# Attention and routed experts on one core: eleven expert tiles start before the last sequence is dispatched

## The chip, the cores and the metric

The kernel runs on one core of one Trainium2 chip. The metric is device microseconds (us) of one execution. A core has TensorE (PE; the rows call its weight loads PEld), VectorE (DVE), ScalarE (ACT), GpSimd (POOL) and SyncE (SP), each with an instruction queue of its own that it works through in order. [...]

## The reference

Four sequences of 768 tokens, 8 heads of 64. First block-sparse attention: query block and key block (of 32) see each other if they are neighbours, if one of them is the first or last, or if the pair was drawn. Then each token goes to the one expert of eight whose embedding is nearest by cosine, and the expert's result is scaled by the gate.

```
scores = scale * q @ k.T;  scores = where(mask, scores, -1e9)
attn   = exp(scores - max) / (sum + 1e-9);  x = attn @ v          # 3072 tokens of 512
logits = (x / |x|) @ (emb / |emb|).T / tau                        # 8 experts
e = argmax(logits);  gate = softmax(logits)[e]
out = gate * (relu(x @ w1[e]) @ w2[e])                            # w1 512x1024, w2 1024x512
```

## The kernel before, in words

Everything is float32, with two matmul passes per product, so the rows count a float32 matmul twice.

**Attention** (`attention_fast`) is one loop over 192 units. Six units, one per 128 keys, make a window: a pair of heads and half of a sequence's queries. Eight windows make a sequence, 32 windows the whole. In unit u TensorE multiplies the exponentials `e` with the values into `av` (`attend_fast`, L311) and computes the scores `sc` of unit u+2 (`score_fast`, L290), of which ScalarE makes `e` (L293). DVE adds the `e` of a window into `esum` (L306, L308). At a window's end ScalarE copies half of `av` to `part` (L315) and DVE adds the other half into `at` (L317). That frees `av`, of which there is one. In the same place `turn_fast` transposes keys and queries of a later pair (L273) into a PSUM tile that DVE and ScalarE read as `kt` (L276) and `qt` (L277).

`settle` (L339, L346 and what follows) turns a finished window into rows of `x`: 12 matmuls `back<-back,at`, 24 matmuls that sum `esum`, then on DVE `dens`, `inv`, `x`, `part`, and `nsq` behind POOL's squares `sq` (L359). It is called in the second unit of the next window (u%6 == 1). After a sequence's last window come `route` (logits, arg-max `oh`, `gate`; a chain of small instructions on DVE, one on POOL, one on ScalarE), in unit 2, and `rank`, in unit 4: how many tokens before a token have the same expert. `rank` adds up `seen` on POOL (L451) and multiplies `rk` on TensorE (L453, L454). The last sequence does all three after the loop.

One PSUM tile, `small`, is shared by the transposes of a turn, `settle`, `rk`, `cp` and `slot_ps` (`two_banks`), one buffer in all.

**Dispatch** (L459) comes after the last `rank`: count per expert, tiles of 128 tokens per expert, a place for every token, and a matmul of one-hot rows that writes the token numbers into `slot`, 24 matmuls with `lane_oh` made on DVE in front of each.

**Experts.** 24 tiles, and up to 7 more behind conditions (three of those run). `fetch(i)` loads w1 and w2 of the tile's expert through SP, three buffers each, and gathers its 128 rows `xg` through POOL. `expert_tile` transposes `xg` (L553), copies it to `xgt` on DVE (L555), multiplies `hp` in two halves (L562), applies relu on ScalarE (L565) and DVE (L566), multiplies `yp` (L570) and scales it on DVE into `y` (L572), which POOL scatters.

The order on each engine is set by a scheduler of the language that lists the instructions by its own estimate of when they become ready. [...]

Of the kernel before, what the change touches and what calls it, by code (L numbers as in the profile page):

```python
# [10 lines left out]
F32 = mybir.dt.float32  # L11
# [7 lines left out]
P = 128  # L19
# [11 lines left out]
GS = G // P  # L31
NG = (N + E * (G - 1)) // G
NS = NG * GS
# [23 lines left out]
def build_consts(k):  # L57
# [342 lines left out]
def route(k, b):  # L400
# [18 lines left out]
    if not k.exact:  # L419
# [39 lines left out]
def dispatch(k):  # L459

    nc, p = k.nc, k.dp
    cp = two_banks(k, "cp")[:, 0]
    nc.tensor.matmul(cp[:, 0:E], lhsT=k.ones, rhs=k.seen[:, NT, :], start=True, stop=True)
    cnt = p.tile([P, E], F32, name="cnt")
    nc.vector.tensor_copy(out=cnt, in_=cp[:, 0:E])

    more = p.tile([P, E, N // G], F32, name="more")
    nc.vector.tensor_tensor(out=more, in0=cnt.unsqueeze(2).broadcast_to([P, E, N // G]),
                            in1=k.by_g.unsqueeze(1).broadcast_to([P, E, N // G]), op=ALU.is_gt)
    need = p.tile([P, E], F32, name="need")  # L470
    nc.vector.reduce_sum(out=need, in_=more, axis=AX.X)
    end = need
    for step in (1, 2, 4):
        nxt = p.tile([P, E], F32, name=f"end{step}")
        nc.vector.tensor_copy(out=nxt[:, 0:step], in_=end[:, 0:step])
        nc.vector.tensor_tensor(out=nxt[:, step:E], in0=end[:, step:E], in1=end[:, 0:E - step], op=ALU.add)
        end = nxt
# [3 lines left out]
    past = p.tile([P, NG, E], F32, name="past")  # L481
    nc.vector.tensor_tensor(out=past, in0=k.tile_no.unsqueeze(2).broadcast_to([P, NG, E]),
                            in1=end.unsqueeze(1).broadcast_to([P, NG, E]), op=ALU.is_ge)
    ex = p.tile([P, NG], F32, name="ex")
    nc.vector.reduce_sum(out=ex, in_=past, axis=AX.X)
    nc.vector.tensor_scalar(out=ex, in0=ex, scalar1=float(E - 1), scalar2=None, op0=ALU.min)
    k.expert = k.const.tile([P, NG], I32, name="expert")
    nc.vector.tensor_copy(out=k.expert, in_=ex)

# [15 lines left out]
    nc.vector.scalar_tensor_tensor(out=low, in0=hi, scalar=-float(P), in1=pos, op0=ALU.mult, op1=ALU.add)
# [246 lines left out]
```

## Time and profile before

| | us |
| --- | --- |
| median of 3 runs (873.19 to 874.57) | 873.22 |
| the profiled execution | 872.45 |
| its span, first to last instruction | 870.6 |
| TensorE busy | 774.4 |
| DVE busy | 328.3 |
| ACT busy | 200.0 |
| POOL busy | 101.1 |

The mean granted clock of TensorE is 0.957 of full speed. A window's row gives the length of a stretch, then busy time and number of instructions per engine. A line of the timeline gives start, duration and instruction, and in brackets how long the engine had idled before it and what ended that. Where one engine is busy for most of a stretch the reader looks for the releaser behind its remaining idle time.

### The profile page before, as it was taken

To read this page: it belongs to the slowest core of one execution; us is meant where nothing else is said; L and a number is where in the kernel's file an instruction comes from. 1 tells how busy PE (TensorE), PEld (TensorE's weight loads), DVE (VectorE), ACT (ScalarE), POOL (GpSimd) and SP (SyncE) were. 2 spreads that over 40 slices of the span, in tenths; PEclk is the share of its full clock that TensorE was granted. 3 is DMA by queue.
4 is the path that set the end of the run, shared out by engine and by line. 5 is a ranking of instruction groups with operands and counts; after the bars stand their busy time and mean duration, and the time that the engine had idled before them with its cause. 6 is when DMAs were issued, how large, how long until landed. Compare 5 with 4: busy or idle time off the path is not lost.

```text
span 870.6 us, 22250 instructions
## 1 busy us (share of the span) xinstructions
PE 774.4 (89%) x10030; PEld 504.6 (58%) x10030; DVE 328.3 (38%) x641; ACT 200.0 (23%) x292; POOL 101.1 (12%) x139
## 2 busy tenths in 40 slices
PE   5999979998799979997459999999999999999883
PEld 2555535555455545553447676767676767676661
DVE  3666656666566665666711111111111111110100
ACT  3545434444344434443000000000000000000000
POOL 2000010001100010001010111101010101010100
PEclk9999989999899989999559999999999999999997
DMA  5111131111111130000179999989999999988780
GB/s 200 39 42 50 43 128 58 57 57 58 74 57 57 58 129 20 3 3 2 72 290 399 399 398 323 330 312 324 323 315 323 322 322 321 326 314 314 272 296 28
DMA packets 63810, 162.31 MB, mean 186 GB/s; under 512 B 2956, under 2 KB 15244, under 8 KB 63190
## 3 DMA queue, kind: packets, MB, share of 16 engines
q1 hardware_dynamic: 58950, 146.45, 47.9%
q0 software_dynamic: 4480, 13.91, 4.0%
q8 instruction: 82, 1.34, 0.6%
q10 hardware_dynamic: 272, 0.39, 0.1%
q14 instruction: 26, 0.21, 0.1%
HBM read 148.14 MB, written 13.38 MB: 186 GB/s over the span
## 4 chain that ended last, share of the span: by engine, by line
PE 73%; DVE 9%; issue 6%; ACT 6%; DMA 2%; POOL 2%; SPq 0%; POOLq 0%; DVEq 0%; ACTq 0%
PE hp L562 20%; PE yp L570 19%; PE sc L290 14%; PE av L311 12%; ACT e L293 3%; DVE esum L306 3%; PE back L346 2%; PE back L339 2%; DVE kt L276 2%; ACT qt L277 2%; PE slot_ps L514 1%; PE xg_ps L553 1%; DMA xg<-x_dram,slot 1%; DMA out_dram<-y,slot 1%; POOL seen L451 1%
## 5 line engine op out<-in xcount | busy, mean ns | idle before, releaser
L562 PEld LDWEIGHTS hp<-xgt,w 128*128 128x128 f32 x1728 | 199.9, 193 | 25.2 <-issue 11.0
L562 PE MATMUL hp<-xgt,w 128*128 128x128 f32 x1728 | 204.7, 277 | 8.8 <-ACT h L565 4.6
L570 PE MATMUL yp<-w,h 128*128 128x512 f32 x432 | 189.9, 592 | 0.0
L293 ACT ACTIVATE e<-sc 128x768 f32<-128x768 f32 x192 | 155.0, 810 | 150.3 <-PE sc L290 150.3
L311 PE MATMUL av<-e,vld 64*64 64x384 f32 x1536 | 162.9, 495 | 1.4 <-ACT e L293 1.0
L290 PE MATMUL sc<-qt,kt 64*64 64x384 f32 x1536 | 160.8, 490 | 0.0
L308 DVE TENSOR_TENSOR esum<-esum,e 128x768 f32<-128x768 f32 x128 | 122.3, 956 | 56.1 <-ACT e L293 53.1
L570 PEld LDWEIGHTS yp<-w,h 128*128 128x128 f32 x432 | 80.0, 190 | 90.4 <-issue 90.4
L565 ACT ACTIVATE h<-hp 128x512 f32<-128x512 f32 x27 | 16.1, 597 | 414.0 <-PE hp L562 399.7
L290 PEld LDWEIGHTS sc<-qt,kt 64*64 64x64 f32 x1536 | 59.3, 135 | 40.8 <-issue 38.7
L311 PEld LDWEIGHTS av<-e,vld 64*64 64x64 f32 x1536 | 53.0, 135 | 47.7 <-ACT e L293 20.7
L572 DVE TENSOR_SCALAR y<-yp,xg 128x512 f32<-128x512 f32 x27 | 20.3, 751 | 158.9 <-PE yp L570 158.9
L566 DVE TENSOR_SCALAR h<-hp 128x512 f32<-128x512 f32 x27 | 18.7, 692 | 161.2 <-PE hp L562 161.2
L573 POOL DMA_INDIRECT out_dram<-y,slot x27 | 27.4, 1016 | 353.5 <-DVE y L572 339.1
L359 POOL TENSOR_TENSOR sq<-x 128x384 f32<-128x384 f32 x32 | 26.4, 826 | 354.5 <-DVE part L361 209.7
L290 PE MATMUL sc<-qmask,kmask 64*64 64x384 bf16 x768 | 67.2, 329 | 0.0
L290 PEld LDWEIGHTS <-kmask 64*64 64x64 bf16 x768 | 24.8, 109 | 33.7 <-issue 33.7
L339 PEld LDWEIGHTS back<-back,at 64*64 64x64 f32 x768 | 14.7, 132 | 45.3 <-ACT qt L277 43.1
L339 PE MATMUL back<-back,at 64*64 64x72 f32 x768 | 19.3, 231 | 24.2 <-ACT qt L277 23.0
L306 DVE TENSOR_TENSOR esum<-e 128x768 f32<-128x768 f32 x32 | 30.7, 958 | 19.3 <-ACT e L293 19.3
L555 DVE COPY xgt<-xg_ps 128x512 f32<-128x512 f32 x27 | 18.5, 687 | 42.3 <-PE xg_ps L553 42.3
L538 POOL DMA_INDIRECT xg<-x_dram,slot x29 | 29.9, 1032 | 30.0 <-PE good_ps L378 21.4
(128 smaller groups left out, 375.4 us busy)
## 6 DMA issues: line engine op xcount, KB each, us to landing
w<-in_moe_w_dram SPq DMA_DIRECT2D x58, 2048.0 KB, 10.3
x_dram<-x SPq DMA_DIRECT2D x4, 1539.0 KB, 5.8
kld<-in_k_dram SPq DMA_DIRECT2D x16, 384.0 KB, 4.8
vld<-in_v_dram SPq DMA_DIRECT2D x16, 384.0 KB, 3.3
qld<-in_q_dram SPq DMA_DIRECT2D x15, 384.0 KB, 5.4
xg<-x_dram,slot POOLq DMA_INDIRECT x29, 7.3
out_dram<-y,slot POOLq DMA_INDIRECT x27, 7.5
qld<-in_q_dram ACTq DMA_DIRECT2D x1, 384.0 KB, 3.3
```

Of the source, the lines that this page charges most:

```text
L290: nc.tensor.matmul(ps[D * r:D * (r + 1), h, 0:HALF], lhsT=rows[D * h:D * (h + 1), keys], rhs=cols[D * h:D * (h + 1), queries], start=first ...
L293: nc.scalar.activation(e, ps[:, :, 0:HALF], ACT.Exp)
L306: nc.vector.tensor_tensor(out=k.esum, in0=k.first, in1=e, op=ALU.add)
L308: nc.vector.tensor_tensor(out=k.esum, in0=k.esum, in1=e, op=ALU.add)
L311: nc.tensor.matmul(k.av[D * h:D * (h + 1), r, 0:HALF], lhsT=v[D * r:D * (r + 1), h, kc, :], rhs=e[D * r:D * (r + 1), h, :], start=(kc == 0 ...
L339: nc.tensor.matmul(rows[D * s:D * (s + 1), t, h, :], lhsT=at[D * h:D * (h + 1), cols], rhs=k.back[D * h:D * (h + 1), j, :], start=True, st ...
L359: nc.gpsimd.tensor_tensor(out=sq, in0=x, in1=x, op=ALU.mult)
L538: nc.gpsimd.indirect_dma_start(out=x[:, :], out_offset=None, in_=k.x_dram[:, :], in_offset=bass.IndirectOffsetOnAxis(ap=k.slot[:, t:t + 1] ...
L562: nc.tensor.matmul(hp[:, f, :], lhsT=w1[:, d, f * P:(f + 1) * P], rhs=xt[:, d, :], start=(d == 0), stop=(d == ND - 1))
L570: nc.tensor.matmul(yp, lhsT=h[:, f, :], rhs=w2[:, f, :], start=(f == 0), stop=(f == NF - 1))
L572: nc.vector.tensor_scalar(out=y, in0=yp, scalar1=x[:, DM:XW], scalar2=None, op0=ALU.mult)
L573: nc.gpsimd.indirect_dma_start(out=k.out[:, :], out_offset=bass.IndirectOffsetOnAxis(ap=k.slot[:, i:i + 1], axis=0), in_=y[:, :], in_offse ...
```

## The change

- `settle` is called in unit 3 of the next window instead of 1, `route` in unit 4 of the next sequence, and `rank` in unit 14.
- Of the first three sequences, 2304 tokens, eleven full tiles are dispatched inside the last sequence's attention, in six steps, `dispatch_early`. Eleven full tiles are there for every input, since at most 127 tokens per expert are left over. Their rows come from a second copy in memory, `x_early`, which `route` writes as well. `fetch` of tiles 0 and 1 is called in unit 177; `wp`, which holds their weights, lives through attention.
- After the last `settle` and `route` the expert tiles begin. `rank` of the last sequence is called after tile 0, the late dispatch of all other tokens (13 tiles, up to 20) after tile 1, its slots after tile 2. As many tiles are computed as before.
- The matrices that fill the slots are bf16, and the one-hot rows are made six chunks at a time; token numbers are split into two parts for that.
- To make room: two buffers instead of three for `k`, `q` and the small pool of attention, one PSUM buffer instead of two for `xg_ps` and `yp`, two `y` instead of four.

```diff
 def route(k, b):
...
-    nc.sync.dma_start(
-        out=k.x_dram[b * S:(b + 1) * S, :].rearrange("(p c) w -> p (c w)", c=NC),
-        in_=x.rearrange("p c w -> p (c w)"),
-    )
+    for dram in (k.x_early, k.x_dram):
+        if dram is k.x_dram or b < EARLY:
+            nc.sync.dma_start(out=dram[b * S:(b + 1) * S, :].rearrange("(p c) w -> p (c w)", c=NC),
+                              in_=x.rearrange("p c w -> p (c w)"))
...
+def split_lanes(k, low, nt):
+    lanes = k.dp.tile([P, nt, P], BF16, name="lanes")
+    for t in range(0, nt, NC):
+        k.nc.vector.tensor_tensor(out=lanes[:, t:t + NC], in0=k.lane.unsqueeze(1).broadcast_to([P, NC, P]),
+                                  in1=low[:, t:t + NC].unsqueeze(2).broadcast_to([P, NC, P]), op=ALU.is_equal)
+    return lanes
...
+def dispatch_early(k):
+    nc, p, nt = k.nc, k.dp, EARLY * NC
+    cnt = count(k, nt)                       # cp, one matmul
+    yield
...
+    k.experts = [tile_experts(k, end, NE, "expert_e")]
...
+    yield
+    pos = of_expert(k, base, nt, "pos")
...
+    yield
+    low, val = split_places(k, pos, nt, NE)
+    yield
+    lanes = split_lanes(k, low, nt)
+    yield
+    k.slots = [fill_slots(k, lanes, val, nt, NE, "slot_e")]
+    yield
...
 def expert_tile(k, i):
...
-    ps = ring(k, "xg_ps", i, 2, k.eps, [P, ND, P])
+    ps = ring(k, "xg_ps", i, 1, k.eps, [P, ND, P])
...
-    yp = ring(k, "yp", i, 2, k.eps, [P, DM])
+    yp = ring(k, "yp", i, 1, k.eps, [P, DM])
...
+    steps = dispatch_early(n)
+    early = [EARLY * per * NPAIR + i for i in (18, 20, 22, 24, 26, 31)]
     for u in range(units):
...
-        if u % NC == 1 and u > NC:
+        if u % NC == 3 and u > NC:
             settle(n, u // NC - 1)
-        if u > NC and u % (per * NPAIR) == 2:
+        if u >= per * NPAIR and u % (per * NPAIR) == 4:
             route(n, u // (per * NPAIR) - 1)
-        if u > NC and u % (per * NPAIR) == 4:
+        if u >= per * NPAIR and u % (per * NPAIR) == 14:
             rank(n, u // (per * NPAIR) - 1)
+        if u in early:
+            next(steps)
+        if u == early[-1] + 2:
+            fetch(n, 0)
+            fetch(n, 1)
         attend_fast(n, u)
...
-    settle(n, units // NC - 1)
-    route(n, B - 1)
-    rank(n, B - 1)
...
+def expert_tiles(n, between=()):
+    between = iter(between)
+    for i in range(NE + NU):
+        if i + 2 == NE:
+            for _ in between:
+                pass
+        fetch(n, i + 2)
+        expert_tile(n, i)
+        next(between, None)
...
+        def between():
+            yield
+            rank(n, B - 1)
+            yield
+            late = dispatch_late(n)
+            next(late)
+            yield
+            next(late)
+            count_good(n)
+            yield
+
+        settle(n, 2 * B * NPAIR - 1)
+        route(n, B - 1)
+        expert_tiles(n, between())
```

The line numbers of the changed kernel differ by a few: L339 is L345 there, L317 is L323, L562 is L658.

DVE's order over one ordinary window, before: the instructions of `settle`, `dens` to `nsq`, come after the first of four further `esum`.

```order
L306 TENSOR_TENSOR esum<-e 128x768
L276 COPY kt<-turn 128x2x3x64
L308 TENSOR_TENSOR esum<-esum,e 128x768
L349 TENSOR_REDUCE dens<-back 128x6
L350 TENSOR_SCALAR dens<-dens 128x6
L352 RECIPROCAL inv<-dens 128x6
L354 TENSOR_TENSOR x<-back,inv 128x3x128
L361 TENSOR_TENSOR part<-back,inv 128x3x16
L360 TENSOR_REDUCE nsq<-sq 128x3
L308 TENSOR_TENSOR esum<-esum,e 128x768 x3
L317 TENSOR_TENSOR at<-av,part 128x384
```

After, the same window of the changed kernel:

```order
L312 TENSOR_TENSOR esum<-e 128x768
L282 COPY kt<-turn 128x2x3x64
L314 TENSOR_TENSOR esum<-esum,e 128x768 x3
L355 TENSOR_REDUCE dens<-back 128x6
L356 TENSOR_SCALAR dens<-dens 128x6
L358 RECIPROCAL inv<-dens 128x6
L360 TENSOR_TENSOR x<-back,inv 128x3x128
L367 TENSOR_TENSOR part<-back,inv 128x3x16
L366 TENSOR_REDUCE nsq<-sq 128x3
L314 TENSOR_TENSOR esum<-esum,e 128x768
L323 TENSOR_TENSOR at<-av,part 128x384
```

`settle`'s six instructions have moved behind two more `esum`; between them and `at` one `esum` is left of three. On TensorE `back` moves in the same way, behind two more pairs of `av` and `sc`.

DVE's order in the window of the first routing, before: `oh` to the `at` of that window, with `rank`'s two instructions between.

```order
L431 TENSOR_TENSOR oh<-pick,mx 128x48
L436 TENSOR_SCALAR gate<-gate 128x6
L437 RECIPROCAL x<-gate 128x6
L308 TENSOR_TENSOR esum<-esum,e 128x768
L455 TENSOR_TENSOR mine<-rk,oh 128x48
L456 TENSOR_REDUCE rank<-mine 128x6
L308 TENSOR_TENSOR esum<-esum,e 128x768
L317 TENSOR_TENSOR at<-av,part 128x384
L306 TENSOR_TENSOR esum<-e 128x768
L276 COPY kt<-turn 128x2x3x64
```

After: the same routing chain, with `rank` gone from it.

```order
L441 TENSOR_REDUCE gate<-l 128x6
L437 TENSOR_TENSOR oh<-pick,mx 128x48
L442 TENSOR_SCALAR gate<-gate 128x6
L443 RECIPROCAL x<-gate 128x6
L323 TENSOR_TENSOR at<-av,part 128x384
L312 TENSOR_TENSOR esum<-e 128x768
L282 COPY kt<-turn 128x2x3x64
```

Before, `at` stood two `esum` and the rank behind the end of the chain; now it follows the chain's last instruction.

TensorE's order where the experts begin, before (`cp` and `slot_ps` are the dispatch; w_0 to w_2 are the weight buffers):

```order
L339 MATMUL back<-back,at 64x72 x12
L346 MATMUL back<-ones,esum 64x1 x24
L453 MATMUL rk<-oh,before 128x48
L454 MATMUL rk<-seen,ones 128x48
L463 MATMUL cp<-seen,ones 128x8
L514 MATMUL slot_ps<-val,lane_oh 128x31 x24
L378 MATMUL good_ps<-good_rows,ones 128x1
L553 MATMUL xg_ps_6238<-ident,xg_6198 128x128 x4
L553 MATMUL xg_ps_6311<-ident,xg_6216 128x128 x4
L553 MATMUL xg_ps_6238<-ident,xg_6234 128x128 x4
L553 MATMUL xg_ps_6311<-ident,xg_6307 128x128 x4
L562 MATMUL hp_6245<-xgt_6243,w_0_6194 128x128 x32
```

After, from the last `settle`; `rk` is the last sequence's `rank`.

```order
L345 MATMUL back<-back,at 64x72 x12
L352 MATMUL back<-ones,esum 64x1 x24
L649 MATMUL xg_ps_6182<-ident,xg_5712 128x128 x4
L658 MATMUL hp_6189<-xgt_6187,w_0_5708 128x128 x16
L649 MATMUL xg_ps_6182<-ident,xg_5730 128x128 x4
L459 MATMUL rk<-oh,before 128x48
L658 MATMUL hp_6189<-xgt_6187,w_0_5708 128x128 x16
L666 MATMUL yp_6225<-w_0_5710,h_6190 128x512 x8
L658 MATMUL hp_6261<-xgt_6259,w_1_5726 128x128 x16
L460 MATMUL rk<-seen,ones 128x48
L649 MATMUL xg_ps_6182<-ident,xg_6178 128x128 x4
L468 MATMUL cp<-seen,ones 128x8
```

The dispatch is gone from between the last `settle` and tile 0; `rk` stands between the halves of tile 0's `hp`, and each gap of the tiles holds the next tile's transposes. In the tiles that follow, the order is `hp` x16, `xg_ps` x4, `hp` x16, `yp` x8; before, some of these gaps hold four `hp` of the next tile:

```order
L570 MATMUL yp_6354<-w_1_6214,h_6319 128x512 x8
L562 MATMUL hp_6245<-xgt_6243,w_2_6230 128x128 x16
L562 MATMUL hp_6318<-xgt_6316,w_0_6194 128x128 x4
L562 MATMUL hp_6245<-xgt_6243,w_2_6230 128x128 x16
L570 MATMUL yp_6281<-w_2_6232,h_6246 128x512 x8
L562 MATMUL hp_6318<-xgt_6316,w_0_6194 128x128 x12
```

The four `hp` of the next tile stand between the two sixteens of this one.

## Rows read from the trace of the kernel before

**Rows 1.** Windows: us; PE, PEld, DVE, ACT, POOL busy; granted clock, DMA share, GB/s.

```profile
150.64:162.12 11.48, 10.72 (x244) 6.10 (x240) 7.39 (x13) 5.61 (x8) 0.83 (x1) 1.00 0.01 3
108.46:127.61 19.15, 13.72 (x248) 7.50 (x244) 10.75 (x29) 5.63 (x9) 4.12 (x8) 0.82 0.40 146
208.05:228.52 20.47, 14.82 (x249) 7.70 (x244) 11.31 (x30) 5.74 (x9) 4.09 (x8) 0.84 0.37 137
308.99:328.56 19.57, 14.17 (x249) 7.60 (x245) 10.80 (x30) 5.74 (x9) 4.09 (x8) 0.83 0.40 143
409.54:461.11 51.57, 25.44 (x137) 23.56 (x137) 21.44 (x78) 0.84 (x2) 7.60 (x12) 0.57 0.49 185
461.11:799.73 338.62, 335.89 (x1922) 243.99 (x1921) 47.46 (x68) 13.73 (x23) 45.94 (x45) 1.00 0.94 336
799.73:870.60 70.87, 51.98 (x270) 34.89 (x268) 7.64 (x11) 1.79 (x3) 7.15 (x7) 0.93 0.58 204
```

**Rows 2.** Lines of PE: busy us, mean ns; idle time before it and releasers.

```profile
L339 PE MATMUL back<-back,at 64*64 64x72 f32 x768 | 19.3, 231 | 24.2 <-ACT qt L277 23.0 <-DVE at L317 1.2
...
L453 PE MATMUL rk<-oh,before 128*128 128x48 f32 x8 | 2.4, 392 | 16.7 <-DVE oh L431 9.5 <-DVE gate L436 7.2
```

**Rows 3.** Timeline of one routed window: start, us, engine, instruction, idle before.

```profile
208.39 0.53 PE L273 MATMUL turn<-ident,qld 64*64 64x64 f32 x24
...
210.60 0.49 ACT L277 ACTIVATE qt<-turn 128x384 f32<-128x384 f32 x1 [1.49 <-DVE kt L276]
...
211.14 0.61 PE L339 MATMUL back<-back,at 64*64 64x72 f32 x24 [0.76 <-ACT qt L277]
...
212.24 0.85 PE L311 MATMUL av<-e,vld 64*64 64x384 f32 x8
...
212.70 0.16 DVE L349 TENSOR_REDUCE dens<-back 128x6 f32<-128x12 f32 x1
...
213.72 0.82 PE L311 MATMUL av<-e,vld 64*64 64x384 f32 x8
...
219.98 0.42 PE L453 MATMUL rk<-oh,before 128*128 128x48 f32 x2 [3.18 <-DVE oh L431]
...
220.04 0.19 DVE L437 RECIPROCAL x<-gate 128x6 f32<-128x6 f32 x1
...
222.11 0.66 PE L454 MATMUL rk<-seen,ones 128*128 128x48 f32 x2 [1.71 <-POOL seen L451]
...
222.70 1.56 PE L311 MATMUL av<-e,vld 64*64 64x384 f32 x8
```

**Rows 4.** Timeline from the last `settle` to tile 0's `yp`.

```profile
408.72 0.82 PE L346 MATMUL back<-ones,esum 64*64 64x1 f32 x48
...
416.35 0.21 DVE L431 TENSOR_TENSOR oh<-pick,mx 128x48 f32<-128x48 f32 x1
...
439.66 1.26 POOL L538 DMA_INDIRECT xg<-x_dram,slot  x1 [21.44 <-PE good_ps L378]
...
461.11 2.31 PE L570 MATMUL yp<-w,h 128*128 128x512 f32 x5
```

**Rows 5.** Timeline of a tile whose gap holds four transposes.

```profile
486.52 0.60 PE L553 MATMUL xg_ps<-ident,xg 128*128 128x128 f32 x4
...
487.37 3.84 PE L562 MATMUL hp<-xgt,w 128*128 128x128 f32 x32 [0.25 <-ACT h L565]
...
502.33 3.84 PE L562 MATMUL hp<-xgt,w 128*128 128x128 f32 x32 [0.25 <-ACT h L565]
```

**Rows 6.** Lines of DVE, columns as in rows 2.

```profile
L572 DVE TENSOR_SCALAR y<-yp,xg 128x512 f32<-128x512 f32 x27 | 20.3, 751 | 158.9 <-PE yp L570 158.9
...
L555 DVE COPY xgt<-xg_ps 128x512 f32<-128x512 f32 x27 | 18.5, 687 | 42.3 <-PE xg_ps L553 42.3
...
L500 DVE TENSOR_TENSOR ge<-pos,by_p 128x768 f32<-128x768 f32 x1 | 1.0, 959 | 0.0
```

**Rows 7.** The page's DMA issues: issuing queue, count, size, us to landing.

```profile
w<-in_moe_w_dram SPq DMA_DIRECT2D x58, 2048.0 KB, 10.3
```

More of the change, by code (lines that the diff above doesn't have):

```diff
@@ L30 @@
 G = 128
-GS = G // P
-NG = (N + E * (G - 1)) // G
-NS = NG * GS
+EARLY = B - 1
+NE = (EARLY * S - E * (G - 1) + G - 1) // G
+NG = (N + E * (G - 1)) // G - NE
+NU = N // G - NE
 XW = DM + 1
@@ L456, in rank, with count @@
     nc.vector.reduce_sum(out=k.rank[:, b * NC:(b + 1) * NC], in_=pick, axis=AX.X)
-def dispatch(k):
-    nc, p = k.nc, k.dp
[L462 to L465, printed above, removed]
+def count(k, chunks):
+    ps = two_banks(k, "cp")[:, 0, 0:E]
+    k.nc.tensor.matmul(ps, lhsT=k.ones, rhs=k.seen[:, chunks, :], start=True, stop=True)
+    cnt = k.dp.tile([P, E], F32, name="cnt")
+    k.nc.vector.tensor_copy(out=cnt, in_=ps)
+    return cnt
@@ new lines, in add_up, with tile_experts @@
+def add_up(k, t):
+    for step in (1, 2, 4):
+        nxt = k.dp.tile([P, E], F32, name=f"end{step}")
+        k.nc.vector.tensor_copy(out=nxt[:, 0:step], in_=t[:, 0:step])
+        k.nc.vector.tensor_tensor(out=nxt[:, step:E], in0=t[:, step:E], in1=t[:, 0:E - step], op=ALU.add)
+        t = nxt
+    return t
+def tile_experts(k, end, tiles, name):
+    nc, p = k.nc, k.dp
+    past = p.tile([P, tiles, E], F32, name="past")
+    nc.vector.tensor_tensor(out=past, in0=k.tile_no[:, 0:tiles].unsqueeze(2).broadcast_to([P, tiles, E]),
+                            in1=end.unsqueeze(1).broadcast_to([P, tiles, E]), op=ALU.is_ge)
+    ex = p.tile([P, tiles], F32, name="ex")
+    nc.vector.reduce_sum(out=ex, in_=past, axis=AX.X)
+    nc.vector.tensor_scalar(out=ex, in0=ex, scalar1=float(E - 1), scalar2=None, op0=ALU.min)
+    expert = k.const.tile([P, tiles], I32, name=name)
+    nc.vector.tensor_copy(out=expert, in_=ex)
+    return expert
@@ new lines, in split_lanes, with fill_slots @@
+def split_lanes(k, low, nt):
[4 more added lines that the diff above has]
+    return lanes
+def fill_slots(k, lanes, val, nt, tiles, name):
+    nc, p = k.nc, k.dp
+    ps = two_banks(k, "slot_ps")[:, 0, 0:2 * tiles]
+    for t in range(nt):
+        nc.tensor.matmul(ps, lhsT=lanes[:, t, :], rhs=val[:, t].rearrange("p i s -> p (i s)"),
+                         start=(t == 0), stop=(t == nt - 1))
+    got = p.tile([P, tiles], F32, name="got")
+    nc.vector.tensor_scalar(out=got, in0=ps[:, 0:tiles], scalar1=-64.0, scalar2=float(N), op0=ALU.mult, op1=ALU.add)
+    nc.vector.tensor_tensor(out=got, in0=got, in1=ps[:, tiles:2 * tiles], op=ALU.subtract)
+    slot = k.const.tile([P, tiles], I32, name=name)
+    nc.vector.tensor_scalar(out=slot, in0=got, scalar1=0.0, scalar2=None, op0=ALU.max)
+    return slot
@@ L471, in dispatch @@
     nc.vector.reduce_sum(out=need, in_=more, axis=AX.X)
[L472 to L477, printed above, removed]
+    end = add_up(k, need)
     k.used = k.const.tile([P, 1], I32, name="used")
     nc.vector.tensor_scalar(out=k.used, in0=end[:, E - 1:E], scalar1=float(NG), scalar2=None, op0=ALU.min)
-    past = p.tile([P, NG, E], F32, name="past")
@@ L482, in dispatch @@
[L482 to L488, printed above, removed]
+    k.experts.append(tile_experts(k, end, NG, "expert_l"))
@@ L653, in attention_exact @@
                 rank(n, (u - 1) // (H * NC) - 1)
-def experts(n, tag=""):
-    n.rings = {}
-    with n.tc.tile_pool(name="wp" + tag, bufs=1) as n.wp, n.tc.tile_pool(name="eps" + tag, bufs=1, space=PSUM) as n.eps:
+def expert_tiles(n, between=()):
[7 more added lines that the diff above has]
+        next(between, None)
+    used = n.nc.values_load(n.used[0:1, 0:1], min_val=0, max_val=NG)
+    with ExitStack() as more:
+        for i in range(NU, NG):
+            more.enter_context(n.tc.If(used > i))
+            if i + 2 < NG:
+                fetch(n, NE + i + 2)
+            expert_tile(n, NE + i)
@@ L659, in experts @@
         fetch(n, 0)
         fetch(n, 1)
[L661 to L670 removed]
+        expert_tiles(n)
 @with_exitstack
```

189 lines of the change are left out of this document (114 added, 75 removed).

## The prediction

> **What bounds the kernel now.** I read the engines' shares first, then the span cut into stages, then in each stage what ends TensorE's idle time, and last the timeline around the three places that the change touches. TensorE is the busiest engine everywhere; what differs is why it pauses. The stages [rows 1]: an ordinary attention window (six units; there are 32 windows) takes 11.48 us, of which TensorE is busy 10.72. The windows in which a sequence's routing falls take 19.15, 20.47 and 19.57, that is 7.67, 8.99 and 8.09 more, 24.75 in all, at a granted clock of 0.82 to 0.84. Between the last attention matmul and the first `yp` lie 51.57 us at clock 0.57, half of them without a matmul. From the first `yp` to the 24th lie 338.62 us, 335.89 busy: 23 tiles of 14.72. The rest, 70.87, holds the last full tile, the conditional ones and the last write.
>
> The idle 0.76 of the ordinary window has one cause [rows 2]: `back` of `settle` waited 30 times, 23.0 us in all, for ScalarE's `qt`. The `small` PSUM tile is single, and the turn before it still occupies it. In the routed windows `rk` waits for DVE's `oh` three times, 9.5 us, and its second half for POOL's `seen` [rows 3].
>
> **The change part by part.** The profiled execution took 872.45 us, 0.77 under the median of 873.22; the sum is made from 872.45, and 0.8 is added at the end.
>
> *Settle two units later.* In the order, `back` now stands behind two more pairs of `av` and `sc`, about 2.9 us of TensorE (a unit is 212.24 to 213.72, 1.48 [rows 3]), while `qt` is over at 211.09, 0.05 before `back` starts. So the 0.76 goes, 30 times: -23.0. What is late next is `at` on DVE, which frees the accumulator for the next window's first `av`. From a settle's start t0, that `av` is due at t0 + 6.14 (settle 1.10, three units 4.35, turn 0.69). DVE meanwhile does the esum of unit 4, five instructions of `settle`, `nsq` after POOL's `sq`, the esum of unit 5 and `at`; added up from dens to `nsq` of the routed window (2.74 us) and 0.96 per esum, `at` ends near t0 + 6.2. I put that wait at 0.1 per window, +3. Sum -20; bounds -23 (no wait) and -15 (0.27 each).
>
> *Routing.* `rank` moves ten units on, so `rk` finds `oh` and `seen` ready: its waits of 3.18 and 1.71 [rows 3] go. But `at` stood behind `rank` in DVE's row with half a window to spare; now it stands right behind the whole routing chain. Before, the reciprocal that ends the chain finished 9.09 us after `back` started (211.14 to 220.23), one esum inside. With 0.6 for the esum that now precedes `dens`, and `at` itself, `at` ends near t0 + 10.5, where the `av` is due at t0 + 6.14: a new wait of 4.4 us, three times. Behind it in TensorE's row stand that `av`, and with it every later score and ScalarE's exponentials. The clock: before, the two waits cost it (1 - 0.84) x 20.47 = 3.3 us per routed window [rows 1]; the `av` behind them took 1.56, against 0.85 ahead of them [rows 3], which is half clock. If 4.4 in one piece does the same, a routed window has 4.4 + 3.3 + 0.5 for `rk` = 8.2 over the plain one, against 8.25 on average before: no gain. If the clock holds, 4.9: a gain of 3.3. I take 1.3 each, -4, between the two; bounds +2 (a wait of 5) and -10.
>
> On this the Trainium skill speaks ("TensorE: Matmul & The Clock Gate", Part 1: The HAM clock gate (the "warmup" mystery)): the half clock is the engine's resting state, and work is what lifts it. By that rule the new wait is no cheaper than the two old ones, and the routed windows give 0 instead of -4, the total 837, inside the forecast's own spread. The trace agrees that idling brings the half level; the ordinary window with its 0.76 stays at 1.00.
>
> *Dispatch inside the last sequence.* New work on TensorE: `cp` stands behind a turn and three of the next four `av` and must wait for the `small` tile until `qt` has read it; in the routed window shown that would be 209.4 to 211.09, 1.7 us, and 0.4 for itself; `slot_ps` waits 0.9 for a `qt` in the same way. Its 18 bf16 matmuls have no row: the 24 of `back` L346 took 0.82, 0.034 each [rows 4], and `rk` 0.39 a record [rows 2]; between 0.6 and 7, and I take 1.3, near the narrow ones, for 22 columns are few. DVE gets 36 instructions: 27 small ones at 0.2 (the reciprocal's 0.19 [rows 3]), six of some 200 elements at 0.3, three of 768 at 0.96 [rows 6], together 10 us in 2.4 windows whose DVE has about 3.3 spare each. It comes in lumps ahead of `at`, and of the `part` read that frees `small` for the turn. All of it could be hidden (0) or reach TensorE (10); I take 6.5, as the lumps sit in front of a single buffer. POOL issues four gathers (1.26 each with gaps [rows 4]), which hold back one `sq`: 0.7. Clock: 2.5, less than one routed window's 3.3. Sum 2.1 + 0.9 + 1.3 + 6.5 + 0.7 + 2.5 = +14; bounds +3 and +22. The weights of tiles 0 and 1, four transfers that landed 10.3 us after their issue before [rows 7], are issued at unit 177, fifteen units or 22 us ahead of the last settle; attention covers them.
>
> *The transition.* Let Z be the end of the last settle's matmuls (409.54). Before, the first `yp` stood at Z + 51.57. Now weights and rows of tile 0 are there: transposes and copy 1.65 (0.60 and 0.69 [rows 5, 6] and two handovers), half of `hp` 3.73 to Z + 5.4, the next transposes to 5.9, and then `rk`, which in the order stands in the middle of tile 0 and waits for `oh`. That ended at 416.56, Z + 7.0 [rows 4]; with the `xgt` copy put into its DVE row, Z + 7.8. Then `rk`, and the other half 3.73: `yp` at Z + 12.0. That removes 39.6; 1 comes back for the clock after the 2 us of idling. -38.6, bounds -41 and -33.
>
> *Expert tiles.* In the order of before about every third gap between the halves of `hp` is filled with four `hp` matmuls of the next tile, and the mean tile is 14.72. Afterwards each gap holds four transposes. A tile of that form is shown: 487.37 to 502.33, 14.96 [rows 5], with 0.25 of waiting for `h` left. 23 x 14.96 = 344.1 against 338.62: +5.5 (0 if the gaps cost nothing). In the first four tiles the gaps also take `rk`, `cp`, 24 `slot_ps` and `good_ps`, and DVE the late dispatch, ahead of `y` and `xgt`: 0.6 + 0.4 + 1.25 + 0.75 = +3, bounds 0 and 10. The single `yp` and `xg_ps` cost nothing, as half of `hp`, 3.73, lies between each copy and the next writer. The number of tiles stays 27.
>
> **Sum:** 872.45 - 20 - 4 + 14 - 38.6 + 5.5 + 3 = 832.4, and 0.8 for the median: **833**.
>
> **The rivals.**
> - *The lumps are hidden.* DVE fits its ten us between the esums, and the clock holds in the routed windows: 3 instead of 14, -10 instead of -4: 816. For it: DVE is idle a third of an ordinary window. Against: `at` and `part` are needed at fixed moments, and each has one buffer.
> - *The vector row is later than I think.* Routing's wait is 6 in place of 4.4 with the clock lost (6 + 3.3 + 0.5 = 9.8 a window against 8.25, +5 in place of -4), and the early dispatch costs 19 in place of 14: 833 + 9 + 5 = 847. For it: DVE runs in order, and one late `at` delays the next esums.
> - *The early tiles aren't early.* If the weights wait on SP behind a row's write, or the gathers behind POOL's queue, the first `hp` waits for a pair of transfers, about 20 us: 853. Against: the experts of the early tiles are known 22 us before they are needed, and the slots before that. That fewer than eleven full tiles come out isn't possible: 2304 tokens leave at most 8 x 127 over.
> - *Slower: single buffers chain every tile.* If each `yp` had to wait for `y` of the tile before (0.75 [rows 6]) and each transpose for its copy (0.69), with handovers about 2 us per tile, 23 tiles give 46: 833 + 46 = 879. It decides as soon as the wait is over 1.7 us per tile. For it: the change leaves one buffer of each. Against: it needs the copy to start more than 3 us late in every tile, on a DVE that is busy 47 us of 339 there [rows 1].
>
> **How the numbers follow.** Chances: the forecast 0.54, hidden lumps 0.18, a later vector row 0.18, tiles not early 0.06, chained tiles 0.04 (a quarter of that at no change). The range 817 to 849 leaves out 853 and 879, and about half of the tenth that the unknown terms add at either end. A measurement of this kernel tells 0.2%, 1.7 us, from no change. Faster 0.96, same 0.01, slower 0.03.
>
> **What would show it.** Right: ordinary windows of 10.7 to 10.9 without the wait for `qt`; routed windows with one TensorE wait of 4 to 5 us for `at` in place of the two for `oh` and `seen`; the first `yp` 12 us behind the last settle, with a wait for `oh` of about 2 in the middle of tile 0; tiles of 14.96 throughout. Wrong: if the ordinary windows stay above 11.2, if the last sequence grows by over 25 us against the others, or if tiles take more than 15.5.

## The result, and the profile after

The changed kernel takes 830.38 us (median of 4 runs, 828.27 to 832.27) against 873.21 of the kernel before: a ratio of 0.9506, 95% interval 0.948 to 0.9532. Predicted were 833, in a range of 817 to 849. The profiled execution took 829.78 with a span of 828.1.

Stages of the changed kernel, columns as in [rows 1]: an ordinary window; the three windows that follow a routing; the windows of units 162, 168 and 174; from the last `settle` to the first `yp`; from the first `yp` to the 24th; the rest.

```profile
39.76:50.49 10.73, 10.73 (x244) 6.13 (x240) 7.31 (x14) 5.62 (x8) 0.83 (x1) 1.00 0.38 113
114.88:132.26 17.38, 13.14 (x244) 6.89 (x240) 10.13 (x26) 6.94 (x11) 3.74 (x8) 0.80 0.45 183
207.88:224.51 16.63, 12.41 (x245) 7.06 (x241) 10.14 (x26) 6.94 (x11) 3.73 (x8) 0.90 0.46 192
300.14:316.76 16.62, 12.41 (x245) 6.99 (x241) 10.14 (x26) 6.94 (x11) 3.71 (x8) 0.90 0.46 192
328.00:343.86 15.86, 11.82 (x246) 8.29 (x238) 13.78 (x44) 6.54 (x9) 0.02 (x1) 1.00 0.41 154
343.86:358.17 14.31, 12.46 (x240) 7.02 (x244) 8.42 (x15) 4.92 (x7) 1.63 (x2) 0.88 1.03 395
358.17:375.48 17.31, 14.32 (x263) 9.55 (x259) 8.00 (x17) 5.58 (x8) 5.42 (x5) 0.90 0.29 84
399.30:411.20 11.90, 11.02 (x75) 10.40 (x75) 6.67 (x26) 0.84 (x2) 3.49 (x8) 0.77 1.03 392
411.20:757.22 346.02, 339.38 (x1960) 245.93 (x1959) 60.53 (x109) 13.73 (x23) 47.86 (x45) 1.00 0.90 315
757.22:828.10 70.88, 51.98 (x270) 34.90 (x268) 7.63 (x11) 1.79 (x3) 7.20 (x7) 0.93 0.59 204
```

The ordinary window lost all of its 0.76 of idle time and is busy from end to end. The routed windows are 16.6 to 17.4 and still have some 4 us without a matmul. The early dispatch sits in three windows of 15.86, 14.31 and 17.31. The way to the first `yp` fell from 51.57 to 11.90, and the 23 tiles grew from 338.62 to 346.02.

TensorE's lines, columns as in [rows 2]:

```profile
L317 PE MATMUL av<-e,vld 64*64 64x384 f32 x1536 | 169.3, 504 | 15.7 <-DVE at L323 15.1 <-ACT e L299 0.6
...
L352 PE MATMUL back<-ones,esum 64*64 64x1 f32 x1536 | 28.5, 192 | 2.3 <-issue 2.2
L345 PE MATMUL back<-back,at 64*64 64x72 f32 x768 | 18.1, 223 | 1.5 <-DVE at L323 1.5
L279 PE MATMUL turn<-ident,kld 64*64 64x64 f32 x768 | 17.8, 224 | 2.5 <-DVE part L367 2.4
```

The wait for `qt` is gone from `back`; the idle time of attention now stands before `av`, for `at`: 15.1 us. Two new entries came with the early dispatch: a turn that waits 2.4 for the `part` read, and 2.2 us before the sums of `settle` with no releaser, which the prediction did not have.

| stretch, from the traces | before | after | difference | predicted |
| --- | --- | --- | --- | --- |
| second window's start to the end of the last `settle` | 381.45 | 370.27 | -11.2 | -20 - 4 + 14 = -10 |
| last `settle` to first `yp` | 51.57 | 11.90 | -39.7 | -38.6 |
| first to 24th `yp` | 338.62 | 346.02 | +7.4 | +8.5 |
| from there to the end | 70.87 | 70.88 | 0 | 0 |
| start to the second window | 28.09 | 29.03 | +0.9 | 0 |

Windows are regular from the second on; where it starts varied between 28.3 and 30.0 in the variants below, so the 0.9 is not put down to the change.

The first routed window of the changed kernel (start, duration, instruction, idle time before it), to be held against [rows 3]:

```profile
118.84 0.19 DVE L443 RECIPROCAL x<-gate 128x6 f32<-128x6 f32 x1
...
119.38 0.56 DVE L323 TENSOR_TENSOR at<-av,part 128x384 f32<-128x384 f32 x1 [0.34 <-ACT part L321]
...
119.99 1.56 PE L317 MATMUL av<-e,vld 64*64 64x384 f32 x8 [4.24 <-DVE at L323]
```

The reciprocal ends the routing chain, `at` follows, and `av` has waited 4.24 for it. The forecast was 4.4.

### The profile page after: what moved, and what is told of

Same layout as the page of the kernel before. It is cut to its first block, busy times and chain, and to the rows that moved or that the text cites. A ratio compares the mean times of both kernels' runs of the same rounds, so it can differ in the third digit from the quotient of the medians.

```text
span 828.1 us, 22309 instructions
## 1 busy us (share of the span) xinstructions
PE 768.2 (93%) x10026; PEld 502.6 (61%) x10026; DVE 332.3 (40%) x669; ACT 200.6 (24%) x292; POOL 103.2 (12%) x138
## 4 chain that ended last, share of the span: by engine, by line
PE 80%; DVE 6%; issue 6%; ACT 3%; DMA 1%; POOL 1%; SPq 0%; POOLq 0%; ACTq 0%
PE hp L658 21%; PE yp L666 20%; PE sc L296 17%; PE av L317 15%; PE turn L279 2%; PE back L352 2%; ACT h L661 2%; DVE esum L314 2%; PE back L345 1%; ACT e L299 1%; DMA out_dram<-y,slot_l 1%; POOL nrm L416 1%; DMA emb<-in_moe_expert_emb_dram 1%; DVE nsq L366 0%; DVE x L360 0%
## 5 line engine op out<-in xcount | busy, mean ns | idle before, releaser
L658 PEld LDWEIGHTS hp<-xgt,w 128*128 128x128 f32 x1728 | 200.5, 193 | 30.2 <-ACT h L661 12.4
L658 PE MATMUL hp<-xgt,w 128*128 128x128 f32 x1728 | 206.7, 278 | 12.7 <-ACT h L661 6.9
L317 PE MATMUL av<-e,vld 64*64 64x384 f32 x1536 | 169.3, 504 | 15.7 <-DVE at L323 15.1
L296 PE MATMUL sc<-qt,kt 64*64 64x384 f32 x1536 | 165.2, 495 | 0.0
L317 PEld LDWEIGHTS av<-e,vld 64*64 64x64 f32 x1536 | 53.0, 135 | 67.6 <-issue 23.7
L296 PEld LDWEIGHTS sc<-qt,kt 64*64 64x64 f32 x1536 | 62.0, 137 | 40.7 <-issue 38.0
L296 PE MATMUL sc<-qmask,kmask 64*64 64x384 bf16 x768 | 69.8, 333 | 0.0
L669 POOL DMA_INDIRECT out_dram<-y,slot_l x16 | 16.4, 1026 | 208.2 <-DVE y L668 193.9
L352 PE MATMUL back<-ones,esum 64*64 64x1 f32 x1536 | 28.5, 192 | 2.3 <-issue 2.2
L669 POOL DMA_INDIRECT out_dram<-y,slot_e x11 | 12.7, 1159 | 136.9 <-DVE y L668 124.3
L352 PEld LDWEIGHTS back<-ones,esum 64*64 64x64 f32 x1536 | 27.1, 137 | 2.8 <-issue 2.8
```

The costliest lines, as they stand in the source:

```text
L296: nc.tensor.matmul(ps[D * r:D * (r + 1), h, 0:HALF], lhsT=rows[D * h:D * (h + 1), keys], rhs=cols[D * h:D * (h + 1), queries], start=first ...
L317: nc.tensor.matmul(k.av[D * h:D * (h + 1), r, 0:HALF], lhsT=v[D * r:D * (r + 1), h, kc, :], rhs=e[D * r:D * (r + 1), h, :], start=(kc == 0 ...
L352: nc.tensor.matmul(sums[D * s:D * (s + 1), t, h, r:r + 1], lhsT=esum[D * r:D * (r + 1), h, cols], rhs=k.ones[D * r:D * (r + 1), 0:1], star ...
L658: nc.tensor.matmul(hp[:, f, :], lhsT=w1[:, d, f * P:(f + 1) * P], rhs=xt[:, d, :], start=(d == 0), stop=(d == ND - 1))
L669: nc.gpsimd.indirect_dma_start(out=k.out[:, :], out_offset=bass.IndirectOffsetOnAxis(ap=slot, axis=0), in_=y[:, :], in_offset=None, bounds ...
```

## The experiments

Each single run has a spread of 2 us to either side (the changed kernel's four runs); what follows is therefore read from the stage that an edit touches. In the edits, `issue_after(x)` puts the instructions of a block behind x in the order of x's engine.

**The three call places alone.** The kernel before with `settle` in unit 3, `route` in 4, `rank` in 14.

```diff
-        if u % NC == 1 and u > NC:
+        if u % NC == 3 and u > NC:
             settle(n, u // NC - 1)
```

> The kernel before with only the three call places moved: settle in unit 3, route in unit 4, rank in unit 14; dispatch and experts as before. The windows of the changed kernel's trace give 30 x 0.75 less in the plain part and 5.0 less in the routed ones: 873.2 - 27.5 = 846. The prediction's own terms for it, -20 and -4, give 849. If the gain of the whole change is in the experts' early start alone, and the shorter windows come from the smaller buffers or anything else in it, this stays at 865 or above.

Measured 846.85. The stretch from the second window to the end of the last `settle` is 354.55 (28.69 to 383.24) against 381.45: -26.9. The ordinary windows took 10.73, the routed ones 17.58, 16.62 and 16.61. With this run the parts separate: the early dispatch costs 370.27 - 354.55 = +15.7 in the changed kernel. The way from the last `settle` to the first `yp` is still 51.96 here, so the early start of the tiles gains 40.1 of it. With the tiles' +7.4 that makes -17.0 by the stages, and -16.5 was measured from this run to the changed kernel.

**The routing chain behind `kt`.**

```diff
-        if u >= per * NPAIR and u % (per * NPAIR) == 4:
-            route(n, u // (per * NPAIR) - 1)
+        if u >= per * NPAIR and u % (per * NPAIR) == 6:
+            route(n, u // (per * NPAIR) - 1, n.kt_ins)
...
+    with ExitStack() as late:               # in route, behind the square root
+        if behind is not None:
+            late.enter_context(k.tc.issue_after(behind))
```

> The changed kernel, with the second half of the routing chain (everything behind POOL's square root) queued on DVE behind the kt of the next window instead of ahead of at. If the routed windows (16.6 to 17.4 us in the changed kernel, against 10.73) are long because at stands behind that chain, the wait of 4.2 us for at falls to about 1 (one reduction of 0.87 and one of 0.2 stay ahead of at), the clock stays at 1.00, and each routed window and the one after take together some 5 us less: 830.4 - 16 = 814 to 817. If DVE's capacity is the limit (10.3 us of work in a window of 10.7), the wait only moves to the turn or the at of the window after, and the gain is under 6 us: 824 to 830.

Measured 816.27. A routed window of this kernel:

```profile
114.85:126.58 11.73, 10.95 (x245) 6.20 (x241) 9.58 (x26) 5.75 (x9) 5.98 (x8) 1.00 0.54 223
```

11.73 in place of 17.38, at clock 1.00, with a remaining wait of 0.7, for `e`; the other two read 11.72 and 11.73, and the windows behind them took 11.23 and 11.24 as in the changed kernel, so the wait did not move on. DVE is busy 9.58 of the 11.73. So the long routed windows come from the place of the chain in the engines' rows, and not from a full DVE. (The chain's one ScalarE instruction moves with it; the edit does not separate DVE's row from ScalarE's.)

**`settle` one unit earlier.**

```diff
-        if u % NC == 3 and u > NC:
+        if u % NC == 2 and u > NC:
             settle(n, u // NC - 1)
...
-        if u >= per * NPAIR and u % (per * NPAIR) == 14:
+        if u >= per * NPAIR and u % (per * NPAIR) == 16:
             rank(n, u // (per * NPAIR) - 1)
```

> The changed kernel with settle one unit earlier (third unit of a window instead of fourth), and rank two units later so that rk does not stand behind settle's reads of the small tile. By the trace, qt is over one unit after the place settle had in the kernel before, less 0.7 us, so ordinary windows stay at 10.73. If the wait for at in the routed windows is the length of the chain counted from settle, it shrinks by the unit, 1.45 us, from 4.2 to 2.8, three times, and some of the lost clock comes back: 824 to 827. If that wait is set by something that does not move with settle, nothing changes: 829 to 832. If the ordinary window were held by qt for longer than shown, windows grow to 10.8 or more and the time to over 832.

Measured 820.5, outside all three. An ordinary window, the first routed one and the one behind it, the second routed one, the third and the one behind it:

```profile
38.98:49.47 10.49, 10.49 (x245) 6.20 (x240) 7.39 (x13) 5.62 (x8) 0.83 (x1) 1.00 0.38 116
101.92:116.92 15.00, 10.94 (x245) 6.13 (x240) 10.71 (x28) 5.75 (x9) 3.83 (x7) 0.98 0.34 108
116.92:128.82 11.90, 11.90 (x244) 7.19 (x240) 7.12 (x13) 5.73 (x8) 1.15 (x3) 0.88 0.59 235
192.50:208.66 16.16, 12.14 (x246) 6.55 (x241) 10.99 (x28) 5.75 (x9) 4.11 (x8) 0.89 0.41 137
282.81:297.72 14.91, 10.89 (x244) 6.11 (x240) 10.65 (x28) 5.75 (x9) 3.73 (x7) 0.99 0.33 108
297.72:309.68 11.96, 11.96 (x245) 7.19 (x240) 7.17 (x13) 5.73 (x8) 1.20 (x3) 0.87 0.59 233
```

The ordinary window fell to 10.49. In the changed kernel its third unit takes 1.63 us in place of 1.45 (41.93 to 43.56), and the changed kernel's rows show why: `e` stands behind `qt` on ScalarE, and the weight load of that unit's `av` waits for it.

```profile
42.31 0.49 ACT L283 ACTIVATE qt<-turn 128x384 f32<-128x384 f32 x1 [1.49 <-DVE kt L282]
...
42.70 0.80 ACT L299 ACTIVATE e<-sc 128x768 f32<-128x768 f32 x1
...
43.55 0.21 PEld L317 LDWEIGHTS av<-e,vld 64*64 64x64 f32 x8 [0.66 <-ACT e L299]
```

A `settle` in that place covers the wait. The routed wait stayed at 4.0 instead of shrinking to 2.8, with another name, three times (4.06, 4.02, 4.02):

```profile
114.20 0.24 ACT L440 ACTIVATE l<-l 128x48 f32<-128x48 f32 x1 [5.03 <-DVE pick L434]
...
114.35 1.49 ACT L299 ACTIVATE e<-sc 128x768 f32<-128x768 f32 x2
...
115.19 0.88 PE L317 MATMUL av<-e,vld 64*64 64x384 f32 x8 [4.06 <-ACT e L299]
```

The routing chain's exponential (L440) stands ahead of that `e` in ScalarE's row. ScalarE idles 5.03 us until DVE's chain has reached `pick`, and `e` starts right behind. So TensorE still waits for the chain, now by way of ScalarE. Whether `e`, which has four buffers that the `esum` set free, would have found one earlier no run tests. The length counted from `settle` was the wrong reading: one queue holds up whatever stands behind it.

**The first gathers later.**

```diff
+        if u == units - 8:
+            n.gather_after = n.sq_ins        # POOL's squares of the last settled window
+            gather(n, 0)
+            gather(n, 1)
...
+        if i < 4 and not k.exact:
+            wait.enter_context(k.tc.issue_after(k.gather_after))
```

> The changed kernel with the first four gathers of rows issued on POOL some 20 us later, behind the squares of the window that ends at unit 179; all else as it was. In the changed kernel TensorE's sums in settle (back, L352) pause five times for 0.44 us with no releaser while POOL issues those gathers (363.5 to 369.0), 3.5 us lost, and the clock falls after it. If the gathers cause it, that pause leaves its place and appears where the gathers now are; the time changes little, by what the clock then costs. If the place in the program causes it (instructions that arrive late behind the slot matmuls), the pause stays where it was, in the settle after slot_ps, and none appears beside the gathers.

Measured 826.02. The window that took 17.31:

```profile
358.83:370.84 12.01, 11.32 (x263) 6.78 (x258) 7.62 (x17) 5.62 (x8) 0.83 (x1) 1.00 0.12 40
```

5.3 us less, at clock 1.00. The pause has left its place, but none appeared beside the gathers: half of the forecast. They now began (380.50) after one `settle`'s sums and ended before the next one's. Two further runs put idle squares on POOL ahead of them, to move them onto those sums.

```diff
+            idle = n.dp.tile([P, HALF], F32, name="idle")
...
+            with n.tc.issue_after(n.sq_ins):
+                for _ in range(5):           # 3 in the second run
+                    n.gather_after = n.nc.gpsimd.tensor_tensor(out=idle, in0=idle, in1=idle, op=ALU.mult).ins
```

> The kernel with the late gathers once more, but with five idle squares on POOL (0.83 us each, into a tile that nobody reads) in front of them, so that the four gathers run beside the next settle's matmuls (back L345 and L352), as they did in the changed kernel, at another place of the program. If gathers that run beside these short matmuls cause the five pauses of 0.44 us, the pauses are back, in this later settle: 3.5 us there and some clock, 829 to 832. If the pauses belong to the first settle behind slot_ps, there are none: 825 to 827.

Measured 827.44, no pause; the squares took 1.29 us each and the first gather began at 385.05, 0.34 before sums that were over in 0.8.

> The kernel before this pair with three idle squares on POOL in place of five. With five, the first gather began as the settle's sums did and those were over in 0.8 us, so that only one gather ran beside them. A square took 1.29 us there; with three the gathers begin some 2.6 us earlier and two of them are out before the sums begin, as in the changed kernel. If gathers beside the sums make TensorE pause, there are now up to five pauses of 0.44 us in that settle; if none come, the place in the program has a part in it.

Measured 827.65, and the pauses are back, four of them, in a `settle` that had none:

```profile
384.40 1.00 POOL L648 DMA_INDIRECT xg<-x_early,slot_e  x1 [0.30 <-issue]
...
385.70 1.11 POOL L648 DMA_INDIRECT xg<-x_early,slot_e  x1 [0.31 <-issue]
386.42 0.31 PE L352 MATMUL back<-ones,esum 64*64 64x1 f32 x5 [0.43 <-issue]
...
387.12 1.24 POOL L648 DMA_INDIRECT xg<-x_early,slot_e  x1 [0.30 <-issue]
...
388.69 0.48 PE L352 MATMUL back<-ones,esum 64*64 64x1 f32 x20 [0.45 <-issue]
```

They fall between 385.99 and 388.69, while POOL issues gathers from 382.83 to 388.36. And with only two gathers in the old place:

```diff
-        if i < 4 and not k.exact:
+        if 1 < i < 4 and not k.exact:
```

> The changed kernel with the gathers of tiles 0 and 1 where they were, behind slot_e, and those of tiles 2 and 3 behind a later window's squares. If each gather on its way holds TensorE up in that settle, the pauses there fall from five to two or three, and the window from 17.3 to about 14.5. If one gather is enough to start a stretch of pauses that ends by itself, all five stay; if the first two are harmless (the pauses began after the second was issued), none.

Measured 824.24. Two pauses are left, of 0.18 and 0.46, and the sums go on once the second gather is through; the window takes 13.04, less than the 14.5 of the first case:

```profile
363.37 1.19 POOL L648 DMA_INDIRECT xg<-x_early,slot_e  x1 [0.30 <-issue]
...
363.94 0.30 PE L352 MATMUL back<-ones,esum 64*64 64x1 f32 x5 [0.18 <-issue]
...
364.69 0.58 PE L352 MATMUL back<-ones,esum 64*64 64x1 f32 x26 [0.46 <-issue]
```

So the place in the program is not the cause: pauses come where a second or later gather is being issued beside these sums, and none begins after the last is out. The one gather beside the sums of the run with five squares made none. In the changed kernel it looks like this:

```profile
365.10 1.18 POOL L636 DMA_INDIRECT xg<-x_early,slot_e  x1 [0.31 <-issue]
...
366.37 0.31 PE L352 MATMUL back<-ones,esum 64*64 64x1 f32 x7 [0.44 <-issue]
...
368.04 1.00 POOL L636 DMA_INDIRECT xg<-x_early,slot_e  x1 [0.31 <-issue]
...
369.31 0.26 PE L352 MATMUL back<-ones,esum 64*64 64x1 f32 x4 [0.42 <-issue]
```

Five pauses from the second gather's start to about the last one's end. What in the chip holds TensorE up there, and whether it is the issuing or the rows on their way, no run shows.

**Two buffers for `xg_ps` again.**

```diff
+    if i % 2 and i > 4 and not k.exact:
+        if "xg_s" not in k.rings:
+            k.rings["xg_s"] = two_banks(k, "xg_s")
+        ps = k.rings["xg_s"][:, 0].rearrange("p (d t) -> p d t", d=ND)
+    else:
+        ps = ring(k, "xg_ps", i, 1, k.eps, [P, ND, P])
```

> The changed kernel in which, from tile 5 on, every second tile uses the small PSUM tile, free by then, for its transposes: two buffers for xg_ps again, yp still one. The order then has four hp of the next tile in every third gap, and six transposes in the others, as before the change. If the longer tiles (14.96 against a mean of 14.72) come from the single xg_ps alone, the tiles from there on return to 14.67 on average, 19 of them, -5.6: 824 to 826. If the single yp has a part in it, less than half of that: 828 to 830.

Measured 826.46. The 19 tiles from the fifth `yp` to the 24th, first in the changed kernel, then here:

```profile
472.89:757.22 284.33, 279.14 (x1594) 201.98 (x1593) 39.87 (x56) 11.35 (x19) 38.20 (x37) 1.00 0.90 313
```

```profile
475.32:753.41 278.09, 277.02 (x1586) 201.28 (x1585) 39.28 (x56) 11.35 (x19) 38.16 (x37) 1.00 0.91 319
```

14.96 against 14.64 a tile, 6.2 less; the same 19 tiles of the kernel before took 14.67. The single `yp`, still in place here, has no part in it. The mean hides two kinds of tile: in the kernel before and here about every third takes 14.07 and the others 14.96, in the changed kernel all take 14.96. By the two rows 4.1 of the 6.2 us is idle time of TensorE (5.2 against 1.1), the wait for `h` in front of `hp`.

**All four together, then the early dispatch spread.**

> The changed kernel with the four edits of the first experiments together: the routing chain's second half behind the next kt, settle in the third unit and rank in unit 16, the first gathers behind the squares of a later window, two xg_ps from tile 5 on. If their gains are in different places they add up: 13.5 (routed windows), 6 (0.24 in some 25 windows), 4 (the pause in settle), 4 to 5.6 (tiles): 830.4 - 28 = 801 to 805. If DVE's queue is shared between them, so that one gain is paid for by another (the chain behind kt delays a settle that now comes a unit earlier), 810 or more.

Measured 798.34, below the forecast. The four edits alone gave 14.1, 9.9, 4.4 and 3.9, in all 32.3; together they give 32.0, so the gains add up. On top of it:

```diff
-    early = [EARLY * per * NPAIR + i for i in (18, 20, 22, 24, 26, 31)]
+    early = [EARLY * per * NPAIR + i for i in (17, 19, 25, 31, 34)]
...
+            with ExitStack() as order:
+                if u != early[0] and u != early[-1]:
+                    order.enter_context(n.tc.issue_after(n.kt_ins))
                 next(steps)
```

> The combination before this one, and the early dispatch spread over the last sequence: cp in the last unit of a window, where the small tile is free; then one piece of DVE work behind each of three kt (17 small ones; the 12 of places; the three lanes), and the slot matmuls in the fifth unit of that last window. The two windows that hold cp and the lumps took 15.86 and 14.31 in the changed kernel, 8.7 over the plain ones, by a wait of 1.65 for qt, 2.39 for the part read and 1.85 for at, and some lost clock. If those waits come from where the work stands in the two queues, all but about 2 goes: 795 to 798. If DVE is simply full (3.4 us of extra work per window with 3.1 free), a wait for at of 1 to 2 us returns in each of the three windows: 800 to 803.

Measured 789.83 (4 runs, 788.55 to 791.63; ratio to the kernel before 0.9049, 0.9034 to 0.9064), the fastest version here, below both cases: 8.5 less than the combination. The windows of units 162, 168 and 174:

```profile
307.92:318.40 10.48, 10.48 (x244) 6.20 (x240) 8.57 (x28) 5.62 (x8) 0.83 (x1) 1.00 0.28 93
318.40:329.85 11.45, 10.73 (x245) 6.30 (x241) 9.97 (x27) 5.72 (x8) 0.83 (x1) 1.00 1.03 400
329.85:342.88 13.03, 11.49 (x262) 6.72 (x258) 11.43 (x21) 5.72 (x8) 0.83 (x1) 1.00 0.60 225
```

The 17 small instructions cost the first of them nothing; the waits for `at` left are 0.72 and 1.22, and the three windows are 3.5 over the plain 10.49 together. In the combination, where the gathers are late already, they were 11.8 over it (13.73, 17.55 and 12.01), in the changed kernel 15.3 over 10.73. DVE is not full; it was the place in its row again. Last, `rk` one tile later:

```diff
             yield
-            rank(n, B - 1)
+            with n.tc.issue_after(n.yp_ins):
+                rank(n, B - 1)
```

> The spread version with the last sequence's rk queued on TensorE behind tile 0's yp instead of between the halves of tile 0's hp. In the spread version rk waits there 1.85 us for oh, with the clock at full level. If that wait is all it costs, the first yp comes 1.85 to 2.4 us earlier and the rest stays: 787 to 788.5. If the late dispatch, which now starts a tile later, makes a later tile wait for its transposes or its xgt, the gain is taken back: 789 to 792.

Measured 791.36 (4 runs, 790.67 to 793.57): no gain. The wait of 1.85 is gone, but in the profiled execution the first half of tile 0 ran in part at half clock (5.97 us for 32 records that take 3.84), and the tile that now holds `rk` and `cp` took 15.41 for 14.96. So the way from the start of the last `settle` to the first `yp` fell from 14.51 to 13.71 only, and the tiles took part of that back.

## Why the prediction was right, step by step

**Ordinary windows, -20, and routing, -4.** Measured together -26.9. The wait for `qt` went as said, 0.75 in each window. The price of 0.1 for a late `at` was not paid: `at` was in time, and the short delay that there is, 0.18 in the third unit, was not foreseen. In the routed windows the new wait stands where the prediction put it, behind the reciprocal, with 4.24, 4.22 and 4.21 for 4.4. They are 20.0 over the plain windows, those with `rank` included, against 25.0 before: -5.0 for -4, which leaves -21.9 for the ordinary ones. For the clock the forecast took about 2 a window, a value chosen between nothing and 3.3 without a row for it. With the wait taken off, 2.4, 1.7 and 1.7 us are left of the three windows' excess over the plain one. The mean clock of the first would say (1 - 0.80) x 17.38 = 3.5, but it counts idle time at the lower level too, and that costs nothing. So the mechanism of both terms was right; the size of the clock's was a good choice and not a result.

**Early dispatch, +14.** Measured +15.7, and close by luck: two errors of opposite sign. `cp` and the lumps on DVE, from the trace:

```profile
331.18 0.36 PE L468 MATMUL cp<-seen,ones 128*128 128x8 f32 x2 [1.65 <-ACT qt L283]
...
343.61 0.20 DVE L367 TENSOR_TENSOR part<-back,inv 128x48 f32<-128x48 f32 x1
...
343.86 0.58 PE L279 MATMUL turn<-ident,kld 64*64 64x64 f32 x24 [2.39 <-DVE part L367]
...
346.64 1.46 PE L317 MATMUL av<-e,vld 64*64 64x384 f32 x8 [1.85 <-DVE at L323]
```

`cp` waits 1.65 for `qt` (predicted 1.7), the turn 2.39 for `part`, `av` 1.85 for `at`: the lumps cost 4.2, where 6.5 was taken. The slot matmuls took 0.60 for 1.3. The term that failed is the gathers': 0.7, priced as a late `sq`, was 3.5, as pauses of TensorE in that `settle`. The clock took (1 - 0.88) x 14.31 + (1 - 0.90) x 17.31 = 3.4 for 2.5.

**Transition, -38.6.** Measured -39.7, the first `yp` at Z + 11.90 for Z + 12.0 and 1 for the clock, and by another way than the one worked out:

```profile
397.94 1.36 PE L352 MATMUL back<-ones,esum 64*64 64x1 f32 x48
...
401.12 5.59 PE L658 MATMUL hp<-xgt,w 128*128 128x128 f32 x32 [0.78 <-DVE xgt L651]
...
406.89 0.21 DVE L437 TENSOR_TENSOR oh<-pick,mx 128x48 f32<-128x48 f32 x1
...
407.25 0.39 PE L459 MATMUL rk<-oh,before 128*128 128x48 f32 x2
...
411.20 3.17 PE L666 MATMUL yp<-w,h 128*128 128x512 f32 x7
```

The first half of `hp` ran mostly at half clock (the stage's clock is 0.77) and ended late enough for `rk` to find `oh` ready, so that there was no wait: one of the signs that were to show the forecast right did not appear. The spread version goes the way that was worked out. Its first half takes its 3.84 for 32 records, `rk` waits the 2 us that were forecast (1.85), and the second half, behind the wait, runs in part at half clock:

```profile
373.16 0.39 PE L462 MATMUL rk<-oh,before 128*128 128x48 f32 x2 [1.85 <-DVE gate L445]
373.39 5.45 PE L678 MATMUL hp<-xgt,w 128*128 128x128 f32 x32
...
378.68 1.88 PE L686 MATMUL yp<-w,h 128*128 128x512 f32 x4
```

There the first `yp` stands 13.3 behind the end of the last `settle`, as the forecast had it with its 1 for the clock. In both kernels `oh` ends 7.6 to 7.8 behind that point (forecast 7.8), and `rk` starts 0.1 to 0.2 after it; a faster first half only waits for it. In the changed kernel the half clock fell into the first half, where it cost next to nothing, so that the 1 was not paid. That the total came within 1.1 us is partly luck.

**Expert tiles, +5.5 + 3.** 21 of the 23 intervals are 14.96 or 14.97 and one 15.02, as forecast. The late dispatch shows in one tile alone, 16.74, behind `good_ps` and an `xgt` that came 1.1 late: +1.8 for +3.

**The rivals.** Chained tiles (879) and late weights (853) did not occur: the tiles kept 14.96, and the first `hp` waited 0.78 for `xgt`, not for weights. The hidden lumps (816) failed on the 4.2 us of waiting and the routed windows; the later vector row (847) on a wait that stayed at 4.2. That the routed windows would gain nothing did not occur either: -5.0. Behind their three waits the granted clock was at the lower level, 0.50 (121 to 124), 0.50 (214 to 217) and 0.54 (306.5 to 309.5), and 1.00 again further on (126 to 129, 218 to 221, 310 to 313). The Trainium skill ("TensorE: Matmul & The Clock Gate", Part 1: The HAM clock gate (the "warmup" mystery)) has the half clock as the resting state, which work lifts; these rows agree. The reading that the prediction gave it beside its own sum, a wait as dear as the two before it, did not come out: 1.7 to 2.4 us were lost behind the waits, against 3.2 in the second routed window of the kernel before (half clock from 222.11 to its end at 228.52).

## What to carry to other kernels

A step that is moved is not cheap because its engine is idle for a third of the time: what counts is which single buffer waits behind it in that engine's row, and putting a chain behind the instruction that frees the buffer (here `at` and `kt`) gave back 14 us without taking any work away. When a release comes early, look for the next thing in the same queue before counting the gain: with `settle` a unit earlier the wait only changed its name from `at` to `e`. Buffers that are taken away cost through the order that they allow, not only through waits: one `xg_ps` less was 0.3 us per tile on average, as every third tile lost its shorter form, with a wait of only some 0.25 per tile to be seen.

## What was not expected of the hardware

- While POOL issued gathers, TensorE's short matmuls (64x64 weights, one column) paused for up to 0.46 us (0.42 to 0.44 in the changed kernel) about every 0.75 us, without a releaser in the trace. The kernels that left the gathers there have five such pauses too (2.1 us with the chain behind `kt`, 2.0 with two `xg_ps`). The gathers of the expert stage, beside long matmuls, show none.
- The same wait of 4.0 to 4.2 us of TensorE left quite different mean clocks: 0.80, 0.90 and 0.90 in the three routed windows of the changed kernel, 0.98, 0.89 and 0.99 with `settle` a unit earlier. The price was much the same all the same. In the latter kernel the clock fell at the window's end, and the windows behind the first and the third ran at 0.88 and 0.87. Both windows taken together, with the wait and two plain windows taken off, 1.9, 1.7 and 1.9 us are left, against 2.4, 1.7 and 1.7; the dearest such window of the other runs, 17.96 with the late gathers, leaves 3.0. A window's mean clock is no measure of the price: it counts idle time and misses what falls behind the window's end.
